# Squared-ReLU attention and a gated feed-forward on one core: the order in which the third batch's keys and values and the last gate/value weights are loaded

## The chip, the cores and the metric

The kernel runs on one core of one Trainium2 chip. The metric is the time of one execution on the device in microseconds (us); smaller is better. A profiled execution gives, beside its own time, a span from its first to its last instruction and the times of every instruction and transfer inside it. All times in this document that name a place ("at 54.30") count from the start of that span.

The five engines are called as the profile calls them: PE (TensorE, matrix products; PEld is its loading of weights), DVE (VectorE), ACT (ScalarE), POOL (GpSimd) and SP (SyncE). Here POOL mostly issues DMAs, and SP issues the transposing DMAs and some stores.

## The reference

Two steps follow each other. For each of 8 batches and 12 heads (448 rows, 64 columns each), attention without a softmax; then a gated feed-forward over all 3584 rows.

```
scores = q @ k.T / sqrt(64)
attn   = maximum(scores, 0) ** 2 / 448
x      = (attn @ v), the 12 heads side by side: 3584 x 768
out    = (maximum(x @ w_gate, 0) * (x @ w_val)) @ w_out      # 768 -> 1536 -> 768
```

All inputs and the output are float32 in memory; the loads convert to bf16 on their way in.

## The kernel before, in words

**What a batch goes through.** Batches are numbered 0 to 7; "the third batch" is batch 2. Keys and queries of a batch are loaded in their natural layout into `kn_b` and `qn_b` (two buffers each; batches from 2 on all use buffer 0, by `natural`, L136). They have to be transposed, into `T_b` (in the trace `kqT`). For batches 0 and 1 PE transposes them (`transposes`, L202). From batch 2 on it is done without PE: `regroup` (L176) is a DVE copy from `kn` into `kr` or from `qn` into `qr`, and `transpose_grouped` (L183) issues transposing DMAs on SP from there into `T_b`. Each batch needs two copies and four transposing DMAs for keys, and as many for queries.

With `T_b` there, PE makes tiles of scores (`tile_of`, L242), ACT and DVE square their ReLU into `attn` (`relu2`, L230), and value passes on PE multiply by `v_b` (L251, in the trace `vn`; two buffers, so batch 2 uses that of batch 0). ACT and DVE evict the result into `x` (`values`, L263: L266 on ACT, L267 on DVE, then the copies of L261).

**The gate and value products.** For each batch, 12 units (`gv_unit`, L302), one for each 128 columns of `w_gate` and `w_val`, make 12 steps of 4 matmuls each and end with an ACT eviction (L320) and a DVE product into `hT` (L321). The weights lie in six chunks of 256 columns (`gv_sb`, loaded by `load_gv`, L162), so that chunk 5 serves the last two units. The output product of a pair of batches (`out_pair`, L355) uses `wo` (loaded by `load_wo`, L167) and some sums of its blocks, which DVE makes ahead of it (`weight_sums`, L341, its instruction at L345).

**What sets the order.** Each engine runs its instructions in the order in which the program writes them; `pin` (L68) keeps that order. The first batch is written out by hand (`first_batch`, L595). From then on a loop (L745) runs over b = 1 to 6: its units are those of batch b - 1, and the attention of batch b and the preparation of the next batches are "events", put between the steps of units by `spread` (L687). An event (u, n) comes before step n of unit u; `last` is the last unit. For b = 1 the first two units are already done in `first_batch`, so that u counts from the third.

The events that matter here, for b = 1: the copies and transposes of batch 2 (`turned`, L707, at L762: keys from (last - 3, 7), queries from (last - 2, 7)), and at (last, 2) the event of L763. That one begins with `hold(2)` (L673), two tiny POOL copies (L676) that read the end of the transposed keys and queries of batch 2: whatever POOL issues behind them waits until the transposes have landed. For b = 2, `load_v(3)` stands at (1, 1), the first two sums of `wo` at (last - 5, 6) and (last - 3, 6), and the copies of batch 3 from (last - 1, 3).

**The loads.** All loads but the first are issued by POOL through `dma_in` (L115). Keys or queries of a batch are two DMAs (`load_nat`, L130: rows 0 to 255 and 256 to 447), values four (`load_v`, L144), a gv chunk two (gate and value), `wo` two. POOL's order before the change is: parts of batch 0; chunks 0 and 1; keys and queries of batch 1; chunks 2 and 3; values of batch 1; chunks 4 and 5 (L578 to L591); then, written after `first_batch`, keys, queries and values of batch 2 (L743, L744); then the event of L763 with `wo` and batch 3's keys and queries; then batch 3's values.

Of the kernel before, what the change touches and what calls it, by code (L numbers as in the profile page):

```python
# [16 lines left out]
def kernel(  # L17
# [24 lines left out]
    B, H, S, D = q.shape  # L42
# [25 lines left out]
    def pin(ins):  # L68
        return tc.keep_in_program_order(ins)
# [20 lines left out]
    kn_b = [const.tile([128, H, 4, D], BF16, name=f"kn{i}") for i in range(NB)]  # L90
    qn_b = [const.tile([128, H, 4, D], BF16, name=f"qn{i}") for i in range(NB)]
# [23 lines left out]
    def dma_in(o, i):  # L115
        pin(nc.gpsimd.dma_start(out=o, in_=i))  # L116
# [13 lines left out]
    def load_nat(dst, src, b, h0, h1):  # L130
        lo = src[b, h0:h1, 0:256, :].rearrange("h (j i) d -> j h i d", i=4)
        hi = src[b, h0:h1, 256:448, :].rearrange("h (j i) d -> j h i d", i=3)
        dma_in(dst[0:64, h0:h1, :, :], lo)
        dma_in(dst[64:128, h0:h1, 0:3, :], hi)

    def natural(b):  # L136

        return b if b < NB else 0

    def load_qk(b, h0=0, h1=H):  # L140
        load_nat(kn_b[natural(b)], k, b, h0, h1)
        load_nat(qn_b[natural(b)], q, b, h0, h1)

    def load_v(b):  # L144
        for c, p in HALVES:
            if b == 0:
                src = v[b].rearrange("(g c h) s d -> c h g s d", c=2, h=2)[c]
                dst = v_b[b % NB][p].rearrange("p (g h) i d -> p h g i d", h=2)
                parts = [(dst[:, h2], src[h2]) for h2 in range(2)]
            else:  # L150
                parts = [(v_b[b % NB][p], v[b, c * HP:c * HP + HP])]
            for dst, src in parts:
                dma_in(dst[:, :, 0:4, :], src[:, 0:256, :].rearrange("g (j i) d -> j g i d", i=4))
                dma_in(dst[:, :, 4:7, :], src[:, 256:448, :].rearrange("g (j i) d -> j g i d", i=3))
# [7 lines left out]
    def load_gv(c):  # L162
        for (_, p), src in zip(HALVES, (moe_w_gate, moe_w_val)):
            f0, n = CHUNKS[c]
            dma_in(gv_sb[c][p], src.rearrange("(h p) f -> p h f", p=64)[:, :, f0:f0 + n])

    def load_wo():  # L167
        for c in range(2):
            rows = moe_w_out[c * (d_ff // 2):(c + 1) * (d_ff // 2), :]
            dma_in(wo_sb[c], rows.rearrange("(kf p) m -> p kf m", p=128))  # L170
# [5 lines left out]
    def regroup(b, t, h):  # L176

        nat, grp = ((kn_b[natural(b)], kr), (qn_b[natural(b)], qr))[t]
        i = slice(2 * h, 2 * h + 2)
        pin(nc.vector.tensor_copy(grp.rearrange("p i (h d) -> p i h d", d=D)[:, i],  # L180
                                  nat.rearrange("p h i d -> p i h d")[:, i]))
# [115 lines left out]
    def new_x(b):  # L297
        x = [xpool.tile([128, HP, S], BF16, name=f"x{n}") for n in range(2)]
        x_of[b] = [quads(t) for t in x]
        return x  # L300
# [40 lines left out]
    def weight_sums(n):  # L341

        o, a, b, op = ((T1, B12, B11, ALU.subtract), (B12, B22, B12, ALU.subtract),
                       (T2, B22, T1, ALU.subtract), (T4, B21, T2, ALU.subtract))[n]
        pin(nc.vector.tensor_tensor(o, a, b, op))  # L345
# [224 lines left out]
    def gv_units(b):  # L570
        b0 = b - b % 2
        if b == b0:
            hT_of[b0] = hpool.tile([128, KF, 2 * S], BF16, name="hT")
        return [gv_unit(b, mf, BEGUN, rotation((BEGUN_IN[mf],))) if b == 0 and mf < 2 else
                gv_unit(b, mf, BEGUN if mf == 0 else STRAIGHT, acc) for mf in range(KF)]
# [12 lines left out]
    load_gv(3)  # L588
    load_v(1)
    load_gv(4)  # L590
    load_gv(5)  # L591

    NT = NQ * NC

# [66 lines left out]
    def values_event(b, qd):  # L661
        return lambda: (values_by_parity if b >= B - 2 else values)(b, qd, sc_later())

    def transposes_event(b, qd):
        return lambda: transpose_quad(b, qd)
# [3 lines left out]
    def hold_unit(b, mf):  # L669

        pin(nc.gpsimd.tensor_copy(flag[:, 2:3], hT_of[b - b % 2][:, mf, b % 2 * S:b % 2 * S + 1]))

    def hold(b):  # L673

        for t in range(2):
            pin(nc.gpsimd.tensor_copy(flag[:, t:t + 1], T_b[b % NB][:, t, HP - 1, S - 1:S]))  # L676
# [30 lines left out]
    def turned(b, units, *at):  # L707

        def piece(t, h):
            regroup(b, t, h)  # L710
            transpose_grouped(b, t, h)
        return [(*step(units, u, n, 5 * h), lambda t=t, h=h: piece(t, h)) for t, (u, n) in enumerate(at) for h in range(2)]

    def stream(b0, b1):

        e = []
        for b in range(b0, b1):
            for n in range(NT):
                if n % NC == 2 and (b, n) != (b0, 2):
                    vb, qd = (b, n // NC - 1) if n > NC else (b - 1, NQ - 1)  # L720
                    e.append((b, n, values_event(vb, qd), NC))
                e.append((b, n, scores_event(b, n), 1))
        return e

    def paced(units, first, behind, events):

        at = [(u, n) for u in range(len(units)) for n in range(len(units[u]))][first:behind]
        gaps = [{(1, 1): 1, (1, NC): 0.35, (NC, 1): 0.75}[a[3], b[3]] for a, b in zip(events, events[1:])]
        gap = len(at) / (sum(gaps) + 1)
        places, due = [], gap / 2  # L730
        for (*_, e, _), g in zip(events, gaps + [0]):
            u, n = at[int(due)]
            places.append((u, min(n, len(units[u]) - 4), e))
            due += g * gap
        return places
# [4 lines left out]
    new_x(0)  # L740
    units = gv_units(0)
    first_batch(units)
    load_qk(2)  # L743
    load_v(2)  # L744
    for b in range(1, B - 1):  # L745
        if b != B - 2:
            new_x(b)
        units = units[2:] if b == 1 else gv_units(b - 1)
        last = len(units) - 1
        if b < B - 3:  # L750
            first, behind = {1: (28, 109), 2: (40, 132)}.get(b, (0, 132))
            events = paced(units, first, behind, stream(b, b + 1))
            events.append((last, 8 if b == 1 else 5, values_event(b, NQ - 1)))
        else:
            todo = [e for e in attention if e[:2] <= ENDS[b]]
            del attention[:len(todo)]
            events = paced(units, 0, 144 if b == B - 3 else 132, todo)
            if b == B - 2:
                events.append((last, 5, values_event(B - 1, NQ - 1)))
        if b == 1:  # L760
            events += [(1, 2 + 4 * qd, transposes_event(1, qd)) for qd in range(NQ)]
            events += turned(2, units, (last - 3, 7), (last - 2, 7))  # L762
            events += [(last, 2, lambda: (hold(2), load_wo(), load_qk(3)))]  # L763
        elif b == 2:
            events += [(1, 1, lambda: load_v(3))]
            events += [(last - 5 + 2 * n, 6, lambda n=n: weight_sums(2 * n)) for n in range(2)]
            events += [(last - 1 + t, 3 + 5 * h, lambda t=t, h=h: regroup(3, t, h)) for t in range(2) for h in range(2)]
            events += [(last, 10, lambda: [transpose_grouped(3, t, h) for t in range(2) for h in range(2)])]
        elif b == 3:
            events += [(2, 1, lambda: (hold_unit(2, 1), hold(3), load_qk(4), load_v(4)))]  # L770
            events += turned(4, units, (6, 1), (7, 1)) + [(8, 4, lambda: (hold(4), load_qk(5)))]
        elif b == 4:
            events += turned(5, units, (3, 1), (4, 1)) + [(5, 4, lambda: (hold(5), load_qk(6), load_v(5))), (last, 9, lambda: load_v(6))]
        elif b == 5:
            events += turned(6, units, (1, 6), (2, 6)) + [(4, 1, lambda: (hold(6), load_qk(7)))]
            events += turned(7, units, (last - 2, 6), (last - 1, 6))
            begun = flat(kn_b[1], 4, S)
            begun = x_of[B - 2] = [[begun[:, 2 * e:2 * e + 2, :]] for e in range(2)]
        elif b == 6:
            events += [(3, 1, lambda: (hold(7), load_v(7)))]  # L780
            new_x(b)
            for e in range(2):
                x_of[b][e][0] = begun[e][0]
            x_of[B - 1] = [quads(flat(t, HP, S)) for t in (kr, qr)]
        spread(units, events)
        if b == 2:
            out_pair(0, flat(kn_b[1], KH, S), [lambda: weight_sums(1), lambda: weight_sums(3)])
        elif b == 4:
            out_pair(2, flat(kn_b[1], KH, S))
# [45 lines left out]
```

## Time and profile before

| | before |
|---|---|
| median of 3 runs | 406.69 us (406.0 to 407.07) |
| the profiled execution, its own time | 406.18 us |
| its span | 404.4 us |
| mean granted PE clock | 0.999 |
| PE weight loads, busy | 274.9 us, 68% |
| DMA queue 0 (loads and stores by POOL) | 28.58 MB, 49.6% of the 16 engines' span |
| DMA queue 1 (transposes and stores by SP) | 13.99 MB, 18.2% |
| queue 8 (program) | 57 packets, 0.93 MB |

How to read the views that the prediction shows. A line of waits is: engine and line that waited, what released it, us in total, how many times, the longest. A line of the chain is: start, duration, what the chain of last releases stood in. A line of a timeline is: start, duration, engine, line, operation, output <- input, count, and in brackets the engine's idle time before it and what ended it. The releaser is inferred: it is the latest event on record before the instruction, and can be another than the one truly waited for. "issue" means that the trace shows nothing that was waited for. The share of a DMA queue is the time that its packets took, over 16 engines and the window, and can go over 100% where packets overlap.

### The profile page before, as it was taken

How to read it: one execution, taken by the hardware profiler on the slowest of the kernel's cores; microseconds unless marked ns; L12 is line 12 of the kernel's file. 1: busy time of each engine (PE TensorE's matmuls, PEld its weight loads, DVE VectorE, ACT ScalarE, POOL GpSimd, SP SyncE). 2: the span in 40 equal slices, each digit the busy share in tenths (PEclk: the TensorE clock that was granted, in tenths of full speed). 3: DMA queues.
4: the chain of work that ended last, by engine and by line, in shares of the span. 5: the costliest groups of instructions: out<-in, count | busy, mean ns of one | idle time of the engine just before them, and what ended most of it. 6: DMA issues, size and time to landing. Idle time of an engine off the chain costs nothing.

```text
span 404.4 us, 16572 instructions
## 1 busy us (share of the span) xinstructions
PE 391.1 (97%) x7376; PEld 274.9 (68%) x7376; DVE 304.5 (75%) x532; ACT 244.0 (60%) x358; POOL 95.8 (24%) x164
## 2 busy tenths in 40 slices
PE   7799999999999999999999999999999999999995
PEld 3467766778776666666677677687677766777664
DVE  5975885599944686787733888988889969997751
ACT  4962983697334876877423889899973233444221
POOL 8934500610124602004344021020002230000230
PEclk9999999999999999999999999999999999999999
DMA  9999999898736795947956559552001350000144
GB/s 153 182 197 195 198 193 138 150 201 115 136 82 178 99 170 86 134 103 94 190 101 170 96 84 137 90 89 34 3 2 33 96 151 3 2 3 3 42 122 113
DMA packets 90983, 44.16 MB, mean 109 GB/s; under 512 B 55424, under 2 KB 89952, under 8 KB 90912
## 3 DMA queue, kind: packets, MB, share of 16 engines
q0 software_dynamic: 51136, 28.58, 49.6%
q1 hardware_dynamic: 39104, 13.99, 18.2%
q8 instruction: 57, 0.93, 0.9%
q10 hardware_dynamic: 672, 0.54, 0.5%
q14 instruction: 14, 0.11, 0.1%
HBM read 47.19 MB, written 11.01 MB: 144 GB/s over the span
## 4 chain that ended last, share of the span: by engine, by line
PE 86%; DVE 5%; DMA 4%; ACT 2%; issue 1%; POOL 0%; DVEq 0%; ACTq 0%
PE ps L72 85%; DMA kn<-in_k_dram 3%; DVE attn L233 2%; ACT r_sb L232 2%; DMA kr<-in_k_dram 1%; PE ps L208 1%; DVE kqT L209 1%; DVE attn L399 0%; ACT g_sb L320 0%; PE ps L217 0%; DVE kn L277 0%; DVE r_sb L616 0%; DVE x L639 0%; DVE hT L321 0%; POOL kn L116 0%
## 5 line engine op out<-in xcount | busy, mean ns | idle before, releaser
L72 PE MATMUL ps<-x,gv 64*64 64x448 bf16 x3552 | 203.3, 349 | 0.4 <-ACT r_sb L232 0.3
L72 PEld LDWEIGHTS <-gv 64*64 64x64 bf16 x4032 | 138.8, 107 | 54.5 <-issue 2.5
L232 ACT ACTIVATE r_sb<-ps 128x896 bf16<-128x896 f32 x167 | 147.7, 930 | 18.7 <-PE ps L72 15.7
L233 DVE TENSOR_TENSOR attn<-r_sb 128x896 bf16<-128x896 bf16 x167 | 102.4, 623 | 30.1 <-ACT r_sb L232 24.4
L72 PE MATMUL ps<-kqT 64*64 64x448 bf16 x672 | 68.3, 352 | 4.6 <-ACT r_sb L232 3.3
L72 PEld LDWEIGHTS <-hT 128*64 128x64 bf16 x1056 | 56.1, 110 | 20.9 <-issue 1.7
L409 POOL DMA_DIRECT2D out_dram<-attn x60 | 31.6, 532 | 155.5 <-DVE attn L399 122.8
L395 ACT ACTIVATE attn<-ps 128x384 f32<-128x384 f32 x64 | 28.9, 451 | 64.0 <-PE ps L72 63.9
L72 PE MATMUL ps<-wo,hT 128*64 128x384 bf16 (+1 forms) x720 | 53.9, 306 | 0.0
L321 DVE TENSOR_TENSOR hT<-ps,g_sb 128x448 bf16<-128x448 f32 x72 | 44.6, 620 | 9.1 <-ACT g_sb L320 8.5
L320 ACT ACTIVATE g_sb<-ps 128x448 bf16<-128x448 f32 x72 | 39.2, 547 | 18.4 <-PE ps L72 18.1
L399 DVE TENSOR_TENSOR attn<-ps,attn 128x384 f32<-128x384 f32 (+1 forms) x48 | 22.8, 504 | 33.4 <-ACT attn L395 19.4
L72 PEld LDWEIGHTS <-kqT 64*64 64x64 bf16 x672 | 27.5, 106 | 19.8 <-issue 9.6
L72 PEld LDWEIGHTS <-vn 64*64 64x64 bf16 (+1 forms) x840 | 30.9, 107 | 14.0 <-issue 3.4
L72 PE MATMUL ps<-attn,vn 64*64 64x448 bf16 x672 | 37.2, 350 | 0.9 <-issue 0.8
L513 ACT ACTIVATE kqT<-ps 128x896 f32<-128x896 f32 x18 | 16.5, 919 | 25.0 <-PE ps L72 25.0
L116 POOL DMA_DIRECT2D vn<-in_v_dram x36 | 23.8, 679 | 23.4 <-PE ps L72 8.8
L676 POOL COPY flag<-kqT 128x1 bf16<-128x1 bf16 x12 | 2.8, 239 | 101.9 <-DMA kqT<-kr 74.1
L72 PE MATMUL ps<-o_ring,hT 128*64 128x384 bf16 (+1 forms) x336 | 25.8, 306 | 0.1
L517 DVE TENSOR_TENSOR kqT<-ps,kqT 128x896 f32<-128x896 f32 x18 | 19.5, 1086 | 5.9 <-PE ps L72 4.2
L266 ACT ACTIVATE x<-ps 128x448 bf16<-128x448 f32 x15 | 8.2, 544 | 15.3 <-PE ps L72 15.3
L261 DVE COPY x<-x 64x896 bf16<-64x896 bf16 x36 | 15.3, 424 | 2.0
(104 smaller groups left out, 284.8 us busy)
## 6 DMA issues: line engine op xcount, KB each, us to landing
out_dram<-attn SPq DMA_DIRECT2D x48, 96.0 KB, 2.5
out_dram<-attn POOLq DMA_DIRECT2D x46, 96.0 KB, 2.4
kn<-in_k_dram POOLq DMA_DIRECT2D x7, 384.0 KB, 6.0
qn<-in_q_dram POOLq DMA_DIRECT2D x7, 384.0 KB, 7.8
vn<-in_v_dram POOLq DMA_DIRECT2D x14, 192.0 KB, 9.5
gv<-in_moe_w_gate_dram POOLq DMA_DIRECT2D x6, 384.0 KB, 11.3
gv<-in_moe_w_val_dram POOLq DMA_DIRECT2D x6, 384.0 KB, 10.9
wo<-in_moe_w_out_dram POOLq DMA_DIRECT2D x2, 1152.0 KB, 12.4
```

What stands on the lines that cost most here:

```text
L72: pin(nc.tensor.matmul(o, lhsT=l, rhs=r, start=start, stop=stop, skip_group_check=True))
L116: pin(nc.gpsimd.dma_start(out=o, in_=i))
L232: pin(nc.scalar.activation(r, src, AF.Relu))
L233: pin(nc.vector.tensor_tensor(dst, r, r, ALU.mult))
L261: pin(nc.vector.tensor_copy(x1[p], x0[other]))
L320: pin(nc.scalar.activation(g_sb, o[0], AF.Relu, scale=float(out_scale)))
L321: pin(nc.vector.tensor_tensor(hT[:, mf, col:col + S], o[1], g_sb, ALU.mult))
L395: pin(nc.scalar.activation(out_of(t, r, c), bank(P, t), AF.Copy))
L399: pin(nc.vector.tensor_tensor(o, bank(Q, t), o, ALU.add))
L409: pin(engines[c].dma_start(out=rows[:, c0:c1, :], in_=src))
L513: pin(nc.scalar.activation(held(n, j), both(PQ[n][0]), AF.Copy))
L517: pin(nc.vector.tensor_tensor(k, both(PQ[n][1]), k, ALU.add))
```

## The change

Only POOL's order of loads changes. Chunk 5 of the gate and value weights, which stood ahead of batch 2's keys, now stands between batch 2's keys and its queries. Batch 2's values, which followed its queries, move into the event of L763, behind `hold(2)` and ahead of `wo`. No instruction is added or taken away, and no size or buffer changes.

```diff
     load_v(1)
     load_gv(4)
-    load_gv(5)
...
     first_batch(units)
-    load_qk(2)
-    load_v(2)
+    load_nat(kn_b[natural(2)], k, 2, 0, H)
+    load_gv(5)
+    load_nat(qn_b[natural(2)], q, 2, 0, H)
...
         if b == 1:
             events += [(1, 2 + 4 * qd, transposes_event(1, qd)) for qd in range(NQ)]
             events += turned(2, units, (last - 3, 7), (last - 2, 7))
-            events += [(last, 2, lambda: (hold(2), load_wo(), load_qk(3)))]
+            events += [(last, 2, lambda: (hold(2), load_v(2), load_wo(), load_qk(3)))]
```

## The prediction

> **What bounds the kernel now.** I read the page first. Its line of busy shares says that TensorE works nearly without a break:
>
> ```profile
> PE 391.1 (97%) x7376; PEld 274.9 (68%) x7376; DVE 304.5 (75%) x532; ACT 244.0 (60%) x358; POOL 95.8 (24%) x164
> ```
>
> So an order of loads can only win where PE stands still. I looked for that in the waits of the stretch that the change touches, 50 to 70 us, and in the chain of work there:
>
> ```profile
> PE ps L72 <- issue: 0.8, 1, 0.8
> DVE attn L233 <- ACT r_sb L232: 0.7, 3, 0.3
> PE ps L72 <- DVE x L267: 0.6, 1, 0.6
> DVE kr L180 <- DMA kn<-in_k_dram: 0.5, 1, 0.5
> PE ps L72 <- ACT r_sb L232: 0.2, 1, 0.2
> ```
>
> ```profile
> 41.09 0.74 POOL kn L116
> 41.82 12.85 DMA kn<-in_k_dram
> ...
> 54.79 0.10 DVE kr L180
> ...
> 57.42 0.55 DVE x L267
> 57.96 0.04 issue
> 58.01 6.74 PE ps L72 x134
> 64.75 0.80 issue
> 65.55 9.46 PE ps L72 x194
> ```
>
> The reader is to see two stalls of PE. One ends at 58.01: the keys of batch 2 (`kn`) land at 54.67, VectorE, which runs its instructions in order, has waited 0.49 us for them since 54.30, and all behind that copy is as much late, up to the eviction L267 that PE waits 0.58 us for. The other is the 0.80 us from 64.75, for which the trace names no releaser. A third wait, 0.21 us on ScalarE at 52.67, is not touched. The chain over the whole run shows PE alone from 65.55 for 169.1 us, so what is won before 65.55 should stay won.
>
> **Part 1: keys ahead of gv chunk 5.** Four DMAs change places in the GpSimd queue. From its timeline:
>
> ```profile
> 37.83 0.75 POOL L116 DMA_DIRECT2D gv<-in_moe_w_gate_dram x1 [0.50 <-DMA gv<-in_moe_w_gate_dram]
> 39.81 0.75 POOL L116 DMA_DIRECT2D gv<-in_moe_w_val_dram x1 [1.23 <-DMA gv<-in_moe_w_val_dram]
> 41.09 1.49 POOL L116 DMA_DIRECT2D kn<-in_k_dram x2 [0.53 <-PE ps L72]
> 42.85 1.49 POOL L116 DMA_DIRECT2D qn<-in_q_dram x2 [0.28 <-PE ps L72]
> ```
>
> Each issue here starts 0.3 to 0.6 us after the eighth load before it has landed (39.81 after 24.74 + 14.8 = 39.5; 41.09 after 26.80 + 13.7 = 40.5), so I read the rule as eight loads in flight; the "PE" in two rows is only the latest event before them. The slots stay and their contents change: keys at 37.83 and 39.81, gv at 41.09 and 41.82. Landings follow in order of issue (gv 49.1 and 51.1, keys 53.2 and 54.7, queries 56.9 and 58.2, values 59.2 to 62.9), and sizes are close (gv 384 + 384 KB, keys 384 + 288 KB). So the keys land at about 49.1 and 51, 3.3 us before DVE asks at 54.30. **The wait of 0.49 us goes.** Next in line for L267 is then its place in DVE's queue: it ends at 57.95 - 0.49 = 57.46, and PE, ready at 57.43, goes on at 57.52. Gain 0.49; it could be 0.58 at most (the whole PE wait) and 0 if DVE met another wait. Its operands are there: the ReLU's tiles end at 54.45 and 55.75 on ScalarE, before DVE takes them at 54.77 and 56.3.
>
> What the gv pair pays: it lands where the keys did, at about 54.7, with 12.1 to 12.9 us from issue. Its first reader is the unit before the last; the gate eviction of the unit ahead of that starts at 59.28, so PE wants chunk 5 at about 59.2, or 58.7 after the gain. Four us of cover; with the slowest gv landing of this run, 15.7 us, 41.82 + 15.7 = 57.5 still holds. Cost 0; without that cover each us late is a us of PE. The queries keep slot and place, land at 58.2 and are wanted at 59.42 - 0.5 = 58.9: 0.7 us of cover, the thinnest here.
>
> **Part 2: values behind the transposes.** Four issues (0.66 us each) leave 45.69 to 51.62 and join the event that begins with two copies on GpSimd (L676), which wait for the transposed keys and queries:
>
> ```profile
> 66.57 0.19 POOL L676 COPY flag<-kqT 128x1 bf16<-128x1 bf16 x1 [14.30 <-DMA kqT<-kr]
> 71.04 0.19 POOL L676 COPY flag<-kqT 128x1 bf16<-128x1 bf16 x1 [4.29 <-DMA kqT<-qr]
> 71.28 1.66 POOL L116 DMA_DIRECT2D wo<-in_moe_w_out_dram x2
> ```
>
> Before, the transposes (SP queue, eight from 55.50) share the DMA engines with the queries' tail until 58.2 and with the values until 62.9; the first lands 7.7 us after its issue, against 2.5 us at 98.70, where no load runs. From first issue to the release it took 15.5 us here, and 11.9 to 14.6 us for the pairs from 98.70 and 171.69. After: first issue about 55.0, load traffic over at 58.2, release at 55.0 + 11.9 to 14.6, that is 67 to 69.6; I take 68, near the first, whose loads were also out of the way.
>
> The values then land from 68 on: 2.7 us of issue, and the 4.7 us that the four took in the ring (58.2 to 62.9), so by about 75. Their first reader is the pass at 83.18, 82 after the gain: 7 us of cover. Behind them in the queue stand `wo`, then keys, queries and values of batch 3. `wo`'s first half landed 10.5 us after the release (71.04 to 81.5); with the values ahead, 68 + 10.5 + 4.7 = 83.2 at most, and DVE asks (L345) at 86.32 - 1.3 = 85.0. Batch 3 then lands 3.0 us earlier and 4.7 later than before by the same sum, at most 2 us late against 8 us of cover (keys 90.2, wanted 98.08). Cost 0 while the release is earlier than about 69.8.
>
> **The 0.80 us.** PE's program comes in 57 packets on queue 8, one for about 259 of its instructions, thus one each 6 to 7 us. In the window of 62 to 64 us the DMA view shows one, among transposes that fill the engines:
>
> ```profile
> q1 hardware_dynamic: 830, 0.20, 199.0%
> q8 instruction: 1, 0.02, 4.3%
> q0 software_dynamic: 18, 0.01, 2.4%
> ```
>
> Between 56 and 62 there is none, though the one before is at 54.8. This one ends at 63.9, its neighbours lie at 67.0 and 71.2: it is late, and PE and its weight loads stop at 64.5 to 64.8 in the middle of seven like passes, whose last operand DVE had written by 63.32. I read it as program that came late because loads and transposes stood on the engines at once, from 55.5 to 62.9. Packets amid transposes alone (101.9 to 103.2, 152.6 to 153.0) or loads alone (16 to 54) go with no PE gap of this kind. After the change the overlap is 55.0 to 58.2. I take the stall as gone, 0.80; its bounds are 0 and, if a late packet hits elsewhere, a loss of 1.08 (the gap of the weight loads at 64.47).
>
> [...]
>
> **The sum.** 0.49 + 0.80 = 1.29 us off the profiled execution's 406.18 (its span of 404.4 and 1.8 around it), so 404.9. That execution is 0.5 under the median of the three timed runs, 406.69; the median of all four is 406.4, and I set the time from it: **405.1 us**.
>
> **Rivals.**
> - A: only the DVE wait goes, the 0.80 has another cause or moves to another packet. For: no view names its releaser. Against: its place beside the one late packet. 406.4 - 0.5 = 405.9. [...]
> - B: the keys come no sooner (the issue at 41.09 did wait for PE), or the queries become the wait at 58.9: nothing is won, 406.4. Against: even keys issued at 41.1 would have no gv chunk 5 ahead of them in the ring; the queries keep their place.
> - C, slower: `wo` becomes the wait. With the values ahead it lands 15.2 us after the release; DVE, over 99% busy from 86 to 94 in the table of stretches, meets L345 at 85.0, and each us late goes through to PE. Should the release stay at 71.04, `wo` lands at 86.2 and eats 1.2 of the gain; it decides from 72.3 on, and at 73.3 the time is 406.4 - 1.3 + 3.5 = 408.6. Against: the transposes lose traffic, they don't gain any. For: the values now wait for two copies, and all loads of 26 us stand in one file behind them. [...]
>
> **Chances.** Forecast 0.58, A 0.19, B 0.06, C 0.17. A measurement of this kernel can tell about 0.3% (1.2 us) from no change. The forecast's 1.29 lies just beyond; I count three quarters of it as faster, since what is left out (the 0.21 us wait on ScalarE, shorter waits for program elsewhere) can only add: 0.44 faster; 0.14 + A + B = 0.39 same; C 0.17 slower. The range: down to 406.4 - 0.58 - 0.80 - 0.21 - 0.5 (the spread of the runs, half) = 404.3; up past A and B and their spread into the near part of C, 407.6. That leaves out the far part of C and a little below.
>
> **What would show it.** Right: no wait of L180 on `kn` at 54; L267 over by 57.5; first transpose landed within about 5 us; the copies L676 done by 69; no "issue" wait of PE near 64; first load of `vn` for batch 2 landed by 75; L345 without a wait on a DMA. Wrong: a PE or DVE wait on `gv` at 59, on `qn` at 59, on `wo` at 85 or on `vn` at 82; release at 71 or later; an "issue" wait of PE in another place.

## The result, and the profile after

| | before | after |
|---|---|---|
| median | 406.35 us (18 executions, 405.29 to 408.58) | 405.07 us (18 executions, 404.46 to 406.48) |
| after over before | | 0.9972, 95% interval 0.996 to 0.9983 |
| the profiled execution: own time, span | 406.18, 404.4 us | 405.62, 403.8 us |

The change wins 0.28%, 1.1 us; its median lies 1.3 under that of before. Two things besides the median matter below. The lowest times are 0.8 apart. And the top has gone: 4 of 18 executions of the kernel before lie above 407, none of the changed one. One slow execution on record, 584.28 us of the version with `wo` first at a granted clock of 0.66, is left out of every figure below.

The waits of the changed kernel from 48 to 72 us, which answer to those shown of before:

```profile
PEld L72 <- issue: 1.4, 4, 0.5
DVE x L267 <- PE ps L72: 1.2, 1, 1.2
DVE attn L233 <- ACT r_sb L232: 0.9, 4, 0.3
ACT r_sb L232 <- PE ps L72: 0.6, 3, 0.2
POOL vn L116 <- issue: 0.3, 1, 0.3
PE ps L72 <- ACT r_sb L232: 0.2, 1, 0.2
```

Both of PE's stalls are gone, the 0.58 us behind L267 and the 0.80 us of "issue"; VectorE no longer waits for `kn`; only the 0.21 us on ScalarE is left, and now L267 waits for PE, not PE for L267. The chain of work runs through the place on PE alone:

```profile
53.89 4.54 PE ps L72 x90
58.43 0.01 issue
58.43 16.57 PE ps L72 x340
```

The order of loads is seen in GpSimd's timeline:

```profile
39.54 0.74 POOL L116 DMA_DIRECT2D kn<-in_k_dram  x1 [0.81 <-DVE hT L321]
41.25 0.74 POOL L116 DMA_DIRECT2D kn<-in_k_dram  x1 [0.96 <-DMA gv<-in_moe_w_val_dram]
42.25 0.75 POOL L116 DMA_DIRECT2D gv<-in_moe_w_gate_dram  x1 [0.26 <-DMA vn<-in_v_dram]
43.09 0.75 POOL L116 DMA_DIRECT2D gv<-in_moe_w_val_dram  x1
...
63.80 0.19 POOL L675 COPY flag<-kqT 128x1 bf16<-128x1 bf16 x1 [18.05 <-DVE attn L233]
69.66 0.19 POOL L675 COPY flag<-kqT 128x1 bf16<-128x1 bf16 x1 [5.67 <-DMA kqT<-qr]
70.15 2.62 POOL L116 DMA_DIRECT2D vn<-in_v_dram  x4 [0.30 <-issue]
```

The keys land at 50.6 and 52.1 and are taken at 55.2; the second release comes at 69.7, 1.4 us sooner than before. Laid instruction by instruction beside the profile of before, PE in this execution is 1.0 us late at its 604th matmul, 0.4 late once the wait on L267 is gone, 0.6 early once the stop near 65 is gone, and 0.6 early at the end. Of the 1.0 us, 0.5 came with the first loads, and 0.5 with a new stop at 39:

```profile
37.68 1.52 PE L72 MATMUL ps<-x,gv 64*64 64x448 bf16 x28
39.58 0.38 PE L72 MATMUL ps<-kqT 64*64 64x448 bf16 x4 [0.38 <-DVE hT L321]
```

The view names a DVE instruction, and PE doesn't need that one: in the kernel before it began the same scores at 38.57, while that product (38.32 to 38.94) still ran. Counted in PE's own program (weight loads and matmuls), this stop stands ahead of instruction 1211, and the one near 65 in the kernel before ahead of 2235: 1024 apart. The packets of queue 8 fit that: this stop ended 1.4 us after the fourth was over (38.14), that one 1.6 us after the eighth (63.95). These are four packets apart, so 256 instructions to a packet; over the whole run PE's 14752 instructions make 259 to each of the 57 packets. That gave the experiments their theory.

### The profile page after: what moved, and what is told of

The parts are those of the page before. It is cut to its first block, busy times and chain, and to the rows that moved or that the text cites. A ratio compares the mean times of both kernels' runs of the same rounds, so it can differ in the third digit from the quotient of the medians.

```text
span 403.8 us, 16572 instructions
## 1 busy us (share of the span) xinstructions
PE 392.3 (97%) x7376; PEld 275.9 (68%) x7376; DVE 304.4 (75%) x532; ACT 243.8 (60%) x358; POOL 95.6 (24%) x164
## 4 chain that ended last, share of the span: by engine, by line
PE 86%; DVE 6%; ACT 5%; DMA 1%; issue 1%; DVEq 0%; ACTq 0%
PE ps L72 85%; ACT r_sb L232 4%; DVE attn L233 2%; DMA kr<-in_k_dram 1%; ACT g_sb L320 1%; PE ps L208 1%; DVE kqT L209 1%; DVE x L261 0%; PE ps L217 0%; DVE attn L399 0%; DVE hT L321 0%; DVE kn L277 0%; DVE r_sb L615 0%; DVE x L638 0%; DVE vn L349 0%
## 5 line engine op out<-in xcount | busy, mean ns | idle before, releaser
L395 ACT ACTIVATE attn<-ps 128x384 f32<-128x384 f32 x64 | 28.8, 450 | 64.0 <-PE ps L72 63.9
L261 DVE COPY x<-x 64x896 bf16<-64x896 bf16 x36 | 15.2, 421 | 2.0
```

What stands on the lines that cost most here:

```text
L261: pin(nc.vector.tensor_copy(x1[p], x0[other]))
L395: pin(nc.scalar.activation(out_of(t, r, c), bank(P, t), AF.Copy))
```

## The experiments

**Theory:** the keys part takes away a wait that is always there; the values part takes away PE's stops for a late block of program at instruction 2235, which come when loads and transposes share the DMA engines. **Rivals:** those stops are chance, or a wait for data; and rival C of the prediction, that `wo` has become the wait.

### One part alone, and both kernels again

Keys alone (the values keep their place):

```diff
     load_nat(qn_b[natural(2)], q, 2, 0, H)
+    load_v(2)
     for b in range(1, B - 1):
...
-            events += [(last, 2, lambda: (hold(2), load_v(2), load_wo(), load_qk(3)))]
+            events += [(last, 2, lambda: (hold(2), load_wo(), load_qk(3)))]
```

> Only the keys of batch 2 go ahead of gv chunk 5; the values stay right behind the queries. Theory of the sum: the wait of VectorE on kn at 54.3 goes, so -0.5 us (0 to -0.6); PE's stop in the value passes near 65 stays (0.8 to 1.0 us), since values and transposes still share the DMA engines from about 55 to 63. In all about -0.1%. Rival (the stop there was chance, and its going in the changed kernel too): the stop is as likely here as anywhere, and the time is that of the changed kernel, -1.1 to -1.3 us. Rival B (keys come no sooner): the wait on kn is still there.

Values alone (against the kernel before):

```diff
     load_qk(2)
-    load_v(2)
...
-            events += [(last, 2, lambda: (hold(2), load_wo(), load_qk(3)))]
+            events += [(last, 2, lambda: (hold(2), load_v(2), load_wo(), load_qk(3)))]
```

> Only the values of batch 2 go behind the transposes; gv chunk 5 stays ahead of the keys. Theory of the sum: the wait on kn stays (0.49 us on VectorE, 0.58 on PE), PE's stop near 65 goes, so -0.8 to -1.0 us, 0.2%. Rival (the stop was chance): the stop is there or not as it falls, and the time is that of before within 0.3 us.

Both kernels unchanged, for a second profile:

> The kernel before once more, for its profile. Theory: PE stops near 65 again, 0.6 to 1.1 us, at the same instruction (the weight load ahead of the last matmuls but three of the value pass), because there a block of program ends and the next comes late through loads and transposes. Rival (chance): no stop there, or one in another place.

> The changed kernel once more, for its profile. Theory: no stop of PE near 65. The stop of 0.38 us at 39.2 in the first profile stands 1024 instructions of PE ahead of the one at 65 in the kernel before, a whole number of blocks if a block is 256; I take it as the same kind of late program, amid loads alone, where the order of loads is still that of before: it should come and go by chance in either kernel. Rival: the changed order brings it, and it is there again at 39.

Measured: keys alone 0.9988 of before (0.9959 to 1.0017), values alone 1.0001 (0.9978 to 1.0025). By the ratios neither part alone can be told from no change, and the intervals are too wide to say whether the parts add up. The 0.8 to 1.0 us that the theory gave the values alone did not show. The single times give a hint, though twelve executions are few for it:

| executions | lowest | mean of the lowest quarter | above 407 us |
|---|---|---|---|
| before, run with both parts alone | 405.28 | 405.57 | 6 of 23 |
| keys alone | 404.58 | 404.86 | 2 of 12, up to 409.8 |
| values alone | 405.23 | 405.27 | 5 of 12, up to 408.8 |
| changed kernel (the kernel before, run with it: 405.29, 405.48, 4 of 18) | 404.46 | 404.58 | 0 of 18 |

By the lowest times, the keys are worth 0.7 us and the values 0.05 to 0.3. What is won beyond that at the median is the upper part. It is gone in the changed kernel and in neither of the parts alone; but how much of it there is changes from one set of runs to the next, since of the kernel before 8 of 22 and 0 of 13 executions lie above 407 in the two later sets.

The first profiles show both halves of it. VectorE's copy of the keys, in the second profile of the kernel before and in the one of values alone:

```profile
56.06 0.56 DVE L180 COPY kr<-kn 128x1536 bf16<-128x1536 bf16 x1 [0.98 <-DMA kn<-in_k_dram]
```

```profile
56.90 0.56 DVE L180 COPY kr<-kn 128x1536 bf16<-128x1536 bf16 x1 [2.12 <-DMA kn<-in_k_dram]
```

The wait on the keys is there each time, and its size varies. And PE's value pass in the profile of keys alone:

```profile
63.81 1.33 PE L72 MATMUL ps<-attn,vn 64*64 64x448 bf16 x24
67.89 0.38 PE L72 MATMUL ps<-attn,vn 64*64 64x448 bf16 x4 [2.75 <-issue]
```

The stop is there again, at the same instruction, and 2.75 us long. But the second profile of the kernel before has none there: in that one PE had waited 1.08 us on L267 and came to the place later.

```profile
PE ps L72 <- DVE x L267: 1.1, 1, 1.1
```

The 0.80 us that I had taken as a fixed term comes and goes. The changed kernel has none there in its second profile either, and none at 39.

### Where in the program PE stops

Keys alone, with 16 more instructions of PE ahead of all its work:

```diff
-        idle_matmuls(bank(6), 12)
+        idle_matmuls(bank(6), 16)
```

> Keys alone, as in the run that showed PE's stop of 2.8 us, with 4 more idle double matmuls ahead of the first transposes, so that PE's program holds 16 instructions more ahead of all its work. If the stop is the end of a block of program, it keeps its place in the program (instruction 2235 of PE) and so comes 8 matmuls earlier in the work: after 16 or 17 matmuls of the value pass, in place of 24. If it is a wait for data (the operand that DVE writes), it stays at the last 4 matmuls. If it is absent (it was absent in one profile of two of the kernel before), nothing follows.

Its timeline of PE:

```profile
37.29 1.14 PE L72 MATMUL ps<-x,gv 64*64 64x448 bf16 x20
38.96 0.57 PE L72 MATMUL ps<-x,gv 64*64 64x448 bf16 x8 [0.53 <-issue]
...
63.60 0.95 PE L72 MATMUL ps<-attn,vn 64*64 64x448 bf16 x16
65.93 0.76 PE L72 MATMUL ps<-attn,vn 64*64 64x448 bf16 x12 [1.38 <-issue]
```

The stop comes after 16 matmuls, 8 sooner in the work and at the same instruction 2235. The one near 39 has moved by 8 matmuls too (after 20 of the 28 that it followed), at instruction 1211, and now that no DVE instruction ends near it the view says "issue". So both belong to the place in the program, not to the data; a wait for an operand of DVE is ruled out.

Two more profiles ask when it comes, and a third asks about the wait on the keys:

> Keys alone once more, for its profile. Theory (values beside transposes bring PE's stop at its instruction 2235): the stop is there again, 0.8 to 3 us; it was there in 3 of 4 profiles with the values at that place, and in none of 6 with the values later. Rival (chance, whatever runs): absent as often as not. No wait on kn either way; the copy of the queries may wait up to 0.5 us, as in the first profile (0.27).

> The kernel before a third time, for its profile. The wait on kn is there again (0.49 and 0.98 us so far), and PE behind it by 0.5 to 1.2 us. The stop at instruction 2235: there in one profile of two so far; by the theory it is likelier than not.

> Values alone once more, for its profile. Wait on kn: there again; if the 2.12 us of the first profile were brought by taking the values out from behind the keys, it is near 2 again; by the theory it is 0.5 to 1.0 as in the kernel before, and the 2.12 was a late execution. No stop at instruction 2235.

Keys alone again: a stop of 2.20 us. The kernel before: 0.8 us, and a wait on `kn` of 0.19. Values alone again: no stop, and 0.94 us on `kn`, as in the kernel before, so that the 2.12 belonged to that execution. Yet in both profiles of values alone PE's wait behind the keys was long, 2.2 and 1.0 us against 0.6, 1.1 and 0.3 in the kernel before; that can hide what the values won, and whether it is chance stays open. Over all profiles, stops at instruction 2235:

| values of batch 2 | profiles | with a stop there |
|---|---|---|
| right behind the queries (before, keys alone, shifted) | 6 | 5: 0.8, 0.8, 1.4, 2.2, 2.75 us |
| later (changed kernel, values alone, and all versions below) | 8 | 0 |

The times of packet 8 on queue 8 say it more plainly than the stops. It was over at 64.0 to 64.5 in the three profiles of the kernel before, at 64.4 to 66.5 in the three with the keys ahead and the values in their old place, and at 59.6 to 62.2 in the other eight. All eleven stops at the two instructions ended 1.3 to 1.6 us after packet 4 or packet 8 was over. In the profile of the kernel before without a stop the packet was as late (64.50), and PE, held up by the keys, went on 1.3 us after it without a pause. So PE's two stalls stand in line: by these profiles, where the packet is late, what is won at the keys is waited out at instruction 2235, and where the keys are late enough, the late packet costs nothing and moving the values alone wins nothing.

The link with the place of the values is shown; that the transposes beside them are what makes the packet late is argued from the DMA view and was not tried by itself. The stop at instruction 1211, near 39, falls amid loads alone and came in 6 of the 14 profiles, of the kernel before as of the changed one, with 0.2 to 0.5 us.

One of these profiles also shows one way in which long times come about. Stretches of keys alone, second profile, with the granted clock in the column after POOL's:

```profile
66.00:67.00 1.00, 0.20 (x5) 0.16 (x8) 0.00 (x0) 0.00 (x0) 0.00 (x0) 1.00 1.11 241
67.00:68.00 1.00, 1.00 (x16) 0.64 (x12) 0.65 (x2) 0.54 (x1) 0.19 (x1) 0.53 1.29 268
68.00:70.00 2.00, 2.00 (x28) 1.36 (x24) 1.38 (x3) 0.54 (x1) 0.00 (x0) 0.50 1.05 99
70.00:72.00 2.00, 2.00 (x44) 1.51 (x40) 0.00 (x0) 0.08 (x1) 0.37 (x2) 0.88 0.35 79
```

After the stop of 2.20 us the clock stood at 0.50 for 3.4 us (67.06 to 70.47), which cost another 1.7 us; that execution took 409.14. After the longer stop of the first profile, 2.75 us, it stayed at 1.00.

### Is wo the wait now?

The second profile of the changed kernel has what rival C speaks of. DVE's sums of `wo`:

```profile
85.62 1.36 DVE L345 TENSOR_TENSOR qn<-wo 128x2304 bf16<-128x2304 bf16 x1 [0.35 <-DMA wo<-in_moe_w_out_dram]
91.70 1.36 DVE L345 TENSOR_TENSOR o_ring<-wo,qn 128x2304 bf16<-128x2304 bf16 x1 [0.99 <-DMA wo<-in_moe_w_out_dram]
```

PE waited 0.9 us behind the second. Laid beside the profile of before, PE was 1.0 us early ahead of the first sum and 0.4 late after the second, so that in this execution `wo` cost 1.4 us, more than had been won. Two versions take that wait away in two ways:

```diff
-            events += [(last - 5 + 2 * n, 6, lambda n=n: weight_sums(2 * n)) for n in range(2)]
+            events += [(last - 4 + 2 * n, 6, lambda n=n: weight_sums(2 * n)) for n in range(2)]
```

> The changed kernel, with the two sums of wo (L345) one unit later in the units of the second batch. The second profile of the changed kernel showed DVE waiting 0.35 and 0.99 us for wo there, and PE 0.9 behind it. Theory (rival C of the prediction is real in some executions): no wait on wo, the upper half of the times comes down, median 0.2 to 0.6 us under that of the changed kernel, some 404.6 to 404.9 where that is at 405.1; the lowest times stay at 404.5. Rival (wo is early enough in most executions): the same as the changed kernel within 0.2 us.

```diff
-    def hold(b):
+    def hold(b, ts=(0, 1)):

-        for t in range(2):
+        for t in ts:
...
-            events += [(last, 2, lambda: (hold(2), load_v(2), load_wo(), load_qk(3)))]
+            events += [(last, 2, lambda: (hold(2, (0,)), load_v(2), hold(2, (1,)), load_wo(), load_qk(3)))]
```

> The changed kernel, with the values behind the transposed keys, not behind the transposed queries: they start near 64 and run beside the queries' transposes until about 69. wo then has nothing ahead of it and starts at the second release, near 70 to 72. Theory: wo lands 3 to 4 us sooner than in the changed kernel, no wait at L345; but loads and transposes share the engines for some 5 us again, so a stop of PE in the next blocks (near 71) can come back: 404.6 to 406.0, with a wider spread. Rival (the overlap does nothing to PE's program): like the version with later sums, no stop.

Sums later: 0.9968 of before (0.9954 to 0.9982), 404.61 to 406.77. Values between: 0.9969 (0.9952 to 0.9986), 404.56 to 406.66. Neither shows a wait on `wo` in its profile, neither has a stop at 2235, and neither can be told from the changed kernel's 0.9972; the lower median that the theory of the first asked for did not come. So `wo` was late in one of the changed kernel's two profiles, and what it costs over many executions is below what these runs can measure. The second expectation was wrong in one point: `wo` did not start sooner. The values were issued from 63.9, the release of the queries came at 73.7 (69.7 in the changed kernel, with no load beside its transposes), and `wo` at 74.0, against 72.7. So with the values beside them the transposes were released 4 us later; PE did not stop.

### What the covers hold

The values behind `wo`, and chunk 5 behind the queries:

```diff
-            events += [(last, 2, lambda: (hold(2), load_v(2), load_wo(), load_qk(3)))]
+            events += [(last, 2, lambda: (hold(2), load_wo(), load_v(2), load_qk(3)))]
```

> The changed kernel, with wo ahead of the values in the queue. This takes the cover of the values away: wo's 2304 KB take 15 us, so that the values land at about 70 + 15 + 4.7 = 89 to 91, and PE's first value pass of batch 2 wants them at 82.4. Theory: PE waits 5 to 8 us there and the time is 410 to 413 us. Rival (the pass is covered by other work, since PE takes gv units between): under 2 us lost. No wait at L345.

```diff
     load_nat(kn_b[natural(2)], k, 2, 0, H)
-    load_gv(5)
     load_nat(qn_b[natural(2)], q, 2, 0, H)
+    load_gv(5)
```

> The changed kernel, with gv chunk 5 behind the queries too, to measure its cover. It takes the queries' slots, issued near 44.3 and 45.0, and so lands near 59 to 60; PE wants it at about 59.5. Theory of the sum (4 us of cover in the changed kernel, all of it used up by 4 us of queries): PE waits 0 to 1.2 us on gv, the time is 0 to +1.2 us against the changed kernel, so 405.0 to 406.3. The queries land 3 to 4 us sooner and their copy has no wait. Rival (chunk 5 is wanted later than I read): nothing is lost.

With `wo` first the time is 1.0158 of before (1.0136 to 1.018), 412.6 to 413.5 us, at the upper end of what was expected, though by another sum: the wait is shorter than the 5 to 8 us of the theory, and a lower clock adds to it. PE's waits and one of its stretches:

```profile
PE ps L72 <- DMA vn<-in_v_dram: 4.6, 2, 3.3
```

```profile
86.00:92.00 6.00, 4.75 (x50) 2.24 (x52) 1.40 (x3) 0.94 (x2) 2.63 (x4) 0.50 1.51 196
```

The wait for the values is 4.6 us; PE's clock is 0.50 from 85.3, within that wait, to 92.1, and PE, 4.4 us behind the profile of before when the pass goes on at 87.6, is 6.5 behind at 92. So the cover of the values in the changed kernel is real, and here being late cost 2 us more than the wait itself.

With chunk 5 behind the queries: 0.9994 of before (0.9974 to 1.0014), 404.61 to 407.92, no wait of PE for `gv` in the profile. The value half landed at 58.2, and PE was in that unit from about 59. The rival holds in that profile: all but some 0.7 us of the cover is used up, and nothing was lost. Whether other executions lose something stays open: the ratio stands 0.2% above the changed kernel's, and the two intervals overlap.

## Why the prediction was right, point by point

**The time and the direction** came out as forecast: 405.1 forecast, 405.07 measured; the sum of 1.29 us against 1.1 by the ratio and 1.3 between the medians. The two places and what ends each stall were right. That the sum came so near is in part luck, since one of its terms was a single value out of 0 to 2.75 us, and since it adds two stalls that stand in line, which holds only when both are taken away.

**Part 1, the wait on the keys: right.** It was there in all five profiles with the keys behind chunk 5 (0.19, 0.49, 0.94, 0.98, 2.12 us) and in none of the nine with the keys ahead. The landing was forecast for 49.1 and 51 and came at 50.6 and 52.1, because the two issues came 1.4 to 1.7 us later than the slots that the forecast kept. The size, 0.49, was one draw of a quantity that varies; the lowest times give 0.7.

**Its covers: right, but one thinner than said.** Chunk 5 landed at 54.1 and 56.1, up to 1.4 later than forecast, with 3 us to spare. The queries landed at 59.66 and were taken at 59.85: 0.2 us of cover in place of 0.7. In keys alone they were 0.27 late.

**Part 2, the release and wo: the release was put too early, and the cost of nothing for wo was wrong.** Forecast 68, from a range of 67 to 69.6; it came at 69.7 and 69.3, in both profiles 13.7 to 13.9 us after the first transpose was issued, where 13 had been taken and the row from 171.69 had 14.6. Rival C's threshold of 69.8 was not reached, and yet `wo` was late in one profile, the one with the earlier release. What decided there was the time from the release to the first half of `wo`, forecast as 15.2: it landed at 83.8 in one profile, 14.2 after the release and 2 us ahead of the sum that reads it, and at 85.6 in the other, 16.3 after it. So the threshold rested on a time that itself varies by 2 us, and the cost was 0 in one execution and 1.4 us in the other.

**The 0.80 us: the late packet held, the size was a draw.** The step treated as a fixed term a stop that, by these profiles, goes with how late the packet is (over at 64.0 to 66.5 with the values in their old place, at 59.6 to 62.2 with them later) and with when PE gets there. PE stopped at instruction 2235 for 0 to 2.75 us with the values beside the transposes and not at all without, so the part's worth is not 0.80 in each execution. The sentence that packets amid loads alone pass with no gap was wrong: the changed kernel's own profile has one at 39, of 0.38 us.

**The rivals.** A was half right: nothing in the views names the releaser, and stops do move, but not to where the change would bring them. B did not come. C came in one profile of two, with 1.4 us there, and can't be seen in the times of the versions that take it away.

## What to carry to other kernels

Where a trace shows an engine stopping with no releaser, or with one it does not need, count the instruction's place in that engine's program, and put some idle instructions ahead of it. Here the stop kept its place (2235) with 16 of them ahead and ended 1.3 to 1.6 us after a packet of program, and moving a bulk load away from the transposes took it away (five profiles of six with it, then none of eight). By these profiles two stalls of one engine that followed each other hid one another here: neither part alone could be told from no change (0.9988 and 1.0001 of before), and both together gave 0.9972. So a part which wins nothing alone may still be needed. A stall read from one profile is one draw (this stop was 0 to 2.75 us long); take a second profile of the kernel before ahead of giving it a size, and compare the lowest times as well as the medians. When a load is moved behind a release, work out what then queues behind it, and measure the release from the rows most like the place.

## What the runs showed of the hardware

- The two places where PE stopped stand 1024 of its instructions apart, and the packets of queue 8 that ended before PE went on, the fourth and the eighth, four packets apart: 256 instructions to a packet in this trace. PE stopped at instruction 2235 in five profiles of six with loads and transposes at once (0.8 to 2.75 us), and at 1211 in six of fourteen with loads alone (0.2 to 0.5 us). The eleven stops ended 1.3 to 1.6 us after the packet was over.
- After a PE stop of 2.20 us the granted clock stood at 0.50 for 3.4 us and cost 1.7 us more; after one of 2.75 us it did not fall; with the 4.6 us of wait on `vn` it stood at 0.50 for 6.8 us, from 85.3 to 92.1. What decides whether the clock falls, and for how long, these runs don't show.
